# Making x's normal form again on GpSimd for the backward rows, with two of w1's loads issued later

## The chip, the cores and the metric

The kernel runs on one core of a Trainium2 chip. Its time is the device time of one execution in microseconds (us). The median of three runs before the change is 361.34 us (360.67 to 362.02). Engines are named as in the profile: PE is TensorE, PEld its weight loads, DVE is VectorE, ACT is ScalarE, POOL is GpSimd, SP is SyncE. SP does no arithmetic here, it only issues DMAs; POOL and ACT issue some too.

## The reference

The kernel computes the forward and the backward pass of a two-part mixer on x, of 2048 rows and 448 columns in bf16:

```
h  = x + irfft2(rfft2(layernorm(x)) * (w_r + i w_i))
h2 = h + transpose(gelu(layernorm(h)^T @ w1 + b1) @ w2 + b2)
```

w1 is 2048x1792 and w2 is 1792x2048. The outputs are h2 and, for a given grad_out, the gradients of x, w_r, w_i, w1, b1, w2 and b2. The layernorm has no weights: each row has its mean taken off and is divided by the root of its variance. The result of layernorm(x), called x's normal form here, is needed twice: as the input of the forward transform, and at the very end, where the gradient is taken back through the first layernorm (a product with the normal form, and a sum of it).

## The kernel before

Rows are dealt to partitions so that partition q holds rows 16q to 16q+15; a tile [128, 16, 448] holds x, and "row h" of the loops is x[:, h, :], 128 rows at once.

**Front (to about 95 us).** x is loaded in four chunks of four rows each (`load_x`, L255), grad_out in two (L292). `Norm.stats` and `Norm.finish` (L316 to L346) take mean and variance of each row on DVE, a square root on ACT, then `rstd` and `nb` (minus mean times rstd) on DVE, and make the normal form xln = x * rstd + nb, some rows on ACT (L345) and some on DVE (L342). `fft_rows` (L362) folds each group of four rows on DVE (L365, L366) and multiplies by a small table on PE (L376). `fft_cols` (L380), `cmul`, `ifft_cols`, `rows_mid` and `rows_out` are the rest of the transform. In the gaps of that chain PE works on `dg(j)` (L531), j = 0 to 13: grad_out times a transposed block of w2, called w2T. Each block comes by a transposing DMA into one of four buffers; `dg(j)` ends by issuing the load of block j+4 (`load_w2T`, L284).

**Order of the loads.** `nxt` (L202) keeps a list, `chain`: each load that goes through it is issued on SP right behind the one before it, so the order in the code is the order in SP's queue, and a load that must wait for its buffer holds all that are behind it. In this order stand: x, grad_out and the first w2T blocks; the tables; hi, di0, kinv, ident (L548 to L552); four stores of the normal form to DRAM, `xln_d` (L553, L554); block 8, block 9, and then what the loop of L594 to L599 issues: the store of the spectrum xs to DRAM (`xs_d`) behind product 6, and the first three chunks of w1 (`load_w1c`, L587, each two DMAs) behind products 5, 9 and 13. A chunk of w1 goes into a big buffer that earlier data must have left.

**Middle (95 to 230 us).** `gelu_in`, `gelu_out`, `gelu_back`, the product with w2 (L691), and the product with w1 transposed (L748), with the second layernorm's backward. PE works without a break here.

**Backward rows (about 280 to 336 us).** After the backward transform's columns the loop of L842 goes through 16 rows. For each one PE makes the row (`rows_mid_twice`, `rows_out`), and `norm_back` (L707) takes it back through the first layernorm, reading x's normal form from a tile `xr` (two buffers of four rows each, loaded from `xln_d` by POOL's queue every fourth row, L846, L847). The result gx is stored by POOL. Between the rows stand products of the weights' gradients: `gw2` (L762) and `gw1` (L801), whose results go from PSUM to tiles s6 and s4 (four buffers together, tag w4) and out by POOL's queue. From row 10 on `grad_w` adds DVE work.

**What sets the order.** The framework orders each engine's instructions at build time by their place in the code and by when it reckons them ready; `tc.issue_after` adds an order by hand. On the chip each engine runs its own list in that order and waits on semaphores. The loads of xr have no order by hand.

Of the kernel before, what the change touches and what calls it, by code (L numbers as in the profile page):

```python
# [11 lines left out]
BF16 = mybir.dt.bfloat16  # L12
F32 = mybir.dt.float32
ALU = mybir.AluOpType
# [3 lines left out]
P = 128  # L18
S = 2048
D = 448  # L20
# [3 lines left out]
NT = 16  # L24
# [111 lines left out]
def kernel(  # L136
# [21 lines left out]
    ve, ac, po, pe = nc.vector, nc.scalar, nc.gpsimd, nc.tensor  # L158

    consts = ctx.enter_context(tc.tile_pool(name="consts", bufs=1))  # L160
# [3 lines left out]
    dram = ctx.enter_context(tc.tile_pool(name="dram", bufs=1, space=bass.MemoryType.DRAM))  # L164

    def slot(i, shape, name):
        return big.tile(shape, BF16, tag=f"s{i}", name=name)
# [7 lines left out]
    def k1(shape, name, dtype=BF16):  # L175
        return ring.tile(shape, dtype, tag="k1", bufs=10, name=name)
# [4 lines left out]
    def col(n, name, dtype=F32):  # L181
        return ring.tile([P, n], dtype, tag=name, bufs=4, name=name)
# [7 lines left out]
    def ld(out, in_, eng=None):  # L190
        return (eng or nc.sync).dma_start(out=out, in_=in_)

    def st(out, in_, eng=None):
        return (eng or po).dma_start(out=out, in_=in_)  # L194
# [7 lines left out]
    def nxt(load, *args):  # L202
        if chain:
            with tc.issue_after(chain[-1].ins):
                chain.append(load(*args))
        else:
            chain.append(load(*args))
# [41 lines left out]
    def rows(ap):  # L249
        return ap.rearrange("(q h) d -> q h d", h=NT)  # L250
# [22 lines left out]
    def table(shape, src, tag=None):  # L273
        t = consts.tile(shape, BF16, name=src, **({"tag": tag} if tag else {}))
        nxt(ld, t[:], hnd[src].ap())
        return t
# [26 lines left out]
    rstd_x = consts.tile([P, NT], F32, name="rstd_x")  # L303
# [1 line left out]
    gb1 = consts.tile([P, NFB], F32, name="gb1")  # L305
    gb2 = consts.tile([P, NT], F32, name="gb2")

    xln_d = dram.tile([P, NT, D], BF16, name="xln_d")
    xs_d = dram.tile([P, 2, XW], BF16, name="xs_d")
    hn_d = dram.tile([S, D], BF16, name="hn_d")  # L310
    hln_d = dram.tile([NT, P, D], BF16, name="hln_d")
# [4 lines left out]
    class Norm:  # L316
        def __init__(self, src, dst, rstd, eps_col, scale, nm):
            self.src, self.dst, self.rstd, self.eps_col, self.scale, self.nm = src, dst, rstd, eps_col, scale, nm

        def stats(self, h):  # L320
            if h % 4 == 0:
                self.mv = col(8, f"mv_{self.nm}")
            bs = col(6, f"bs_{self.nm}")
            ve.bn_stats(out=bs[:], in_=self.src[:, h, :])  # L324
            i = h % 4
            ve.bn_aggr(out=self.mv[:, 2 * i:2 * i + 2], in_=bs[:])
            if h % 4 == 3:
                self.finish(h // 4)

        def finish(self, g):  # L330
            mv = self.mv[:, :].rearrange("p (i c) -> p i c", c=2)
            r = self.rstd[:, 4 * g:4 * g + 4]
            sq = col(4, f"sq_{self.nm}")
            ac.activation(out=sq[:], in_=mv[:, :, 1], func=ACT.Sqrt, bias=self.eps_col[:], scale=self.scale)
            ve.reciprocal(out=r, in_=sq[:])
            nb = col(4, f"nb_{self.nm}")
            ve.scalar_tensor_tensor(out=nb[:], in0=mv[:, :, 0], scalar=-1.0, in1=r, op0=ALU.mult, op1=ALU.mult)
            for i in range(4):
                h = 4 * g + i

                if (i > 1 or g == 3) if self.nm == "x" else (i > 1 and g == 3):
                    ve.tensor_scalar(out=self.dst[:, h, :], in0=self.src[:, h, :], scalar1=self.rstd[:, h:h + 1],  # L342
                                     scalar2=nb[:, i:i + 1], op0=ALU.mult, op1=ALU.add)
                else:
                    ac.activation(out=self.dst[:, h, :], in_=self.src[:, h, :], func=ACT.Identity,  # L345
                                  scale=self.rstd[:, h:h + 1], bias=nb[:, i:i + 1])  # L346
# [137 lines left out]
    def rows_mid_twice(ab, itab, h):  # L484

        pq = ps_sp([P, 2, 2, 113])
        for i, (kind, c) in enumerate(((0, 0), (0, 1), (1, 1), (1, 0))):
            last = pe.matmul(pq[:, i // 2, i % 2, :], lhsT=ab[:, kind, c, h, :, :],
                             rhs=itab[:, 113 * i:113 * i + 113], start=True, stop=True)
        eo = k1([P, 2 * DF], "eo2")  # L490
        out = eo[:].rearrange("p (a d) -> p a d", a=2)
        od = f2([P, 2, 113], "od")
        ac.copy(out=od[:], in_=pq[:, :, 1, :])
        ve.tensor_tensor(out=out[:, :, 0:113], in0=pq[:, :, 0, :], in1=od[:], op=ALU.add)
        ve.tensor_tensor(out=out[:, :, 224:112:-1], in0=pq[:, :, 0, 0:112], in1=od[:, :, 0:112], op=ALU.subtract)
        return eo, last
# [13 lines left out]
    def rows_out(eo):  # L510
        py = ps_sp([P, D])
        pe.matmul(py[:, 0:DF], lhsT=kinv[:, 0, :], rhs=eo[:, 0:DF], start=True, stop=False)
        pe.matmul(py[:, DF:D], lhsT=kinv[:, 0, :], rhs=eo[:, 223:0:-1], start=False, stop=False)
        pe.matmul(py[:, 0:DF], lhsT=kinv[:, 1, :], rhs=eo[:, DF:2 * DF], start=False, stop=False)
        pe.matmul(py[:, DF:D], lhsT=kinv[:, 2, :], rhs=eo[:, DF + 223:DF:-1], start=False, stop=True)  # L515
        return py


    xln = slot(1, [P, NT, D], "xln")
    nx = Norm(x, xln, rstd_x, eps_x, 1.0, "x")  # L520
# [10 lines left out]
    def dg(j):  # L531
        pg = ps_mm([P, D])
        with tc.issue_after(folded[min(j - 1, 3)][0].ins) if j else nullcontext():
            for t in range(NT):
                pe.matmul(pg[:], lhsT=w2T[j][:, t, :], rhs=go_nat[:, t, :], start=(t == 0), stop=(t == NT - 1))  # L535
        ev(du[:, j, 0:D], pg[:], "a")
        load_w2T()
# [12 lines left out]
    di0 = table([P, 4 * DF], "di0", "di")  # L550
    kinv = table([P, 3, P], "kinv")
    ident = table([P, P], "ident")  # L552
    for g in range(4):  # L553
        nxt(ld, xln_d[:, 4 * g:4 * g + 4, :], xln[:, 4 * g:4 * g + 4, :])  # L554
    with tc.issue_after(folded[3][1].ins):
        neg(hf[:, 0, 2], hf[:, 0, 1])
    xs = slot(3, [P, 2, XW], "xs")
# [29 lines left out]
    def load_w1c(on):  # L587
        c = len(w1c)
        n = 512 if c < 3 else 256
        w1c.append(slot((2, 4, 6, 5)[c], [P, NT, n], f"w1c{c}"))  # L590
        for k in range(0, n, 256):
            on(ld, w1c[c][:, :, k:k + 256], w1v[:, :, 512 * c + k:512 * c + k + 256])

    for j in range(4, NFB):  # L594
        dg(j)
        if j == 6:
            nxt(ld, xs_d[:], xs[:])
        if j in (5, 9, 13):
            load_w1c(nxt)  # L599


# [83 lines left out]
    for t0 in range(0, NT, 4):  # L685
# [7 lines left out]
        for i in range(4):  # L693
# [3 lines left out]
                                    op0=ALU.add, op1=ALU.add)  # L697
# [9 lines left out]
    def norm_back(ps, mean, xhat, rstd_c, back, base, out):  # L707

        v = f2([P, D], "v")
        if mean:  # L710
            nm1 = col(1, "nm1")
            ac.activation(out=nm1[:], in_=ps[:, D:D + 1], func=ACT.Copy, scale=rstd_c)  # L712
            ac.activation(out=v[:], in_=ps[:, 0:D], func=ACT.Identity, scale=rstd_c, bias=nm1[:])
        else:
            ac.activation(out=v[:], in_=ps[:, 0:D], func=ACT.Copy, scale=rstd_c)
        nm2 = col(1, "nm2")
        junk = k1([P, D], "junk")
        ve.tensor_tensor_reduce(out=junk[:], in0=v[:], in1=xhat, scale=back, scalar=0.0,
                                op0=ALU.mult, op1=ALU.add, accum_out=nm2[:])
        ve.scalar_tensor_tensor(out=junk[:], in0=xhat, scalar=nm2[:], in1=v[:], op0=ALU.mult, op1=ALU.add)  # L720
        ve.tensor_tensor(out=out, in0=junk[:], in1=base, op=ALU.add)
# [96 lines left out]
    def gw1_four(h):  # L818
        outs, out = gw1(h, ps_mm)
        outer(outs[:2], outs[2:], hlnT, du_t)  # L820
        out()
# [20 lines left out]
    for h in range(NT):  # L842
        if h + 2 < NT:
            mids.append(rows_mid_twice(ab2, di1, h + 2))
        if h % 4 == 0:
            xr = ring.tile([P, 4, D], BF16, tag="xr", bufs=2, name="xr")  # L846
            ld(xr[:], xln_d[:, h:h + 4, :], po)  # L847
        with tc.issue_after(mids[-1][1].ins):
            py = rows_out(mids[h][0])
        gx = k1([P, D], "gx")  # L850
        norm_back(py, False, xr[:, h % 4, :], rstd_x[:, h:h + 1], -1.0 / D, dh[:, h, :], gx[:])
        st(rows(out_1[0])[:, h, :], gx[:])
        if h < 8:
            gw2(h + 6, "aaav")
        else:
            gw1_four(h - 8)
        if h == 7:
            ld(xs_b[:], xs_d[:])
        if h > 9:
            grad_w(R_GROUPS[h - 10])  # L860

    for h in range(8, NT, 2):
        outs, out = gw1(h, ps_mm)
# [34 lines left out]
```

## Time and profile before

| | us |
|---|---|
| median of three runs | 361.34 (360.67 to 362.02) |
| the profiled execution's own time | 361.35 |
| its span, from the first instruction to the last | 359.5 |
| PE busy | 334.7 (93% of the span) |
| DVE busy | 243.9 (68%) |
| ACT busy | 210.5 (59%) |
| POOL busy, almost all of it issuing DMAs | 58.1 (16%) |

| stretch, us | PE busy | DVE busy | DMA, GB/s |
|---|---|---|---|
| 0 to 10.9 | 0.02 | 5.59 | 276 |
| 10.9 to 27.5 | 16.02 of 16.60 | 14.12 | 245 |
| 27.5 to 55.2 | 27.54 of 27.70 | 16.94 | 293 |
| 55.2 to 59 | 0.26 of 3.80 | 2.17 | 276 |
| 59 to 73 | 14.00 of 14.00 | 12.53 | 284 |
| 73 to 95 | 21.25 of 22.00 | 15.34 | 262 |
| 280 to 310 | 29.62 of 30.00 | 26.02 | 216 |
| 310 to 335 | 24.74 of 25.00 | 21.70 | 240 |

A line of a view of waits reads: who waited, for whom, us in total, how many times, the longest. A line of a timeline reads: start and length in us, engine, line of the code, operation, what it writes and reads, how often, and in brackets how long the engine stood idle before it and what ended that. A line of a tile's view gives the shortest, the median and the longest duration in ns. SPq is SP's queue of issues. For a DMA the view of its tile also gives the time from issue to landing; landing times below are the issue's start and that time added.

Landings in the front, in us: x's four chunks 4.77, 8.34, 14.45, 15.81; grad_out's two 7.22 and 10.83; w2T block 0 12.69, blocks 1 to 4 17.81, 21.14, 23.07, 25.93; ident 49.39; the four stores to xln_d 50.45, 51.52, 52.60, 53.77; block 8 58.69; the first two xr loads 57.19 and 58.68.

### The profile page before, as it was taken

How to read it: one execution, taken by the hardware profiler on the slowest of the kernel's cores; microseconds unless marked ns; L12 is line 12 of the kernel's file. 1: busy time of each engine (PE TensorE's matmuls, PEld its weight loads, DVE VectorE, ACT ScalarE, POOL GpSimd, SP SyncE). 2: the span in 40 equal slices, each digit the busy share in tenths (PEclk: the TensorE clock that was granted, in tenths of full speed). 3: DMA queues.
4: the chain of work that ended last, by engine and by line, in shares of the span. 5: the costliest groups of instructions: out<-in, count | busy, mean ns of one | idle time of the engine just before them, and what ended most of it. 6: DMA issues, size and time to landing. Idle time of an engine off the chain costs nothing.

```text
span 359.5 us, 5818 instructions
## 1 busy us (share of the span) xinstructions
PE 334.7 (93%) x2100; PEld 184.9 (51%) x2115; DVE 243.9 (68%) x580; ACT 210.5 (59%) x429; POOL 58.1 (16%) x106
## 2 busy tenths in 40 slices
PE   0799996999999999999999999989999999999994
PEld 0456664666664555555555555544555545454442
DVE  4883776967773999822226887837799997599600
ACT  2574653446658999304703344678766666677573
POOL 1000010001113011330160000010100243335620
PEclk9999999999999999999999999999999999999998
DMA  8999999999699999999999888599293365956664
GB/s 280 265 230 335 241 282 279 283 259 299 206 332 263 320 330 261 319 354 312 214 241 217 173 181 164 201 213 200 89 250 99 142 234 188 352 195 249 239 255 154
DMA packets 132988, 87.18 MB, mean 243 GB/s; under 512 B 92032, under 2 KB 124032, under 8 KB 132576
## 3 DMA queue, kind: packets, MB, share of 16 engines
q1 hardware_dynamic: 124768, 56.48, 65.8%
q0 software_dynamic: 8048, 30.31, 23.4%
q8 instruction: 16, 0.26, 0.3%
q14 instruction: 12, 0.10, 0.1%
q10 hardware_dynamic: 144, 0.03, 0.0%
HBM read 32.52 MB, written 30.76 MB: 176 GB/s over the span
## 4 chain that ended last, share of the span: by engine, by line
PE 71%; DVE 12%; ACT 7%; DMA 7%; issue 2%; ACTq 0%; DVEq 0%
PE ps_mm L224 13%; PE ps_mm L748 12%; PE ps_mm L622 6%; PE ps_sp L691 6%; PE ps_mm L691 6%; DMA w2T<-in_B_w_dram 6%; PE ps_mm L535 6%; PE ps_sp L622 5%; PE ps_mm L231 3%; PE ps_sp L224 2%; ACT s L243 2%; DVE bs_x L324 1%; PE ps_sp L405 1%; ACT zt L243 1%; PE ps_sp L376 1%
## 5 line engine op out<-in xcount | busy, mean ns | idle before, releaser
L243 ACT CAST s<-ps_mm 128x512 bf16<-128x512 f32 x96 | 48.4, 568 | 20.1 <-PE ps_mm L231 13.1
L535 PE MATMUL ps_mm<-go_nat,w2T 128*128 128x448 bf16 x224 | 50.9, 361 | 4.1 <-DMA w2T<-in_B_w_dram 4.1
L748 PE MATMUL ps_mm<-du,w1T 128*128 128x449 bf16 x224 | 43.4, 353 | 0.0
L224 PE MATMUL ps_mm<-goT,g_t 128*128 128x512 bf16 x158 | 41.2, 379 | 0.6 <-issue 0.3
L691 PEld LDWEIGHTS <-w2c 128*128 128x128 bf16 x224 | 21.9, 98 | 20.5
L748 PEld LDWEIGHTS <-w1T 128*128 128x128 bf16 x224 | 21.7, 97 | 20.7
L622 PEld LDWEIGHTS <-w1c 128*128 128x128 bf16 x224 | 21.8, 98 | 19.9 <-issue 1.0
L535 PEld LDWEIGHTS <-w2T 128*128 128x128 bf16 x224 | 21.8, 99 | 20.0 <-DMA w2T<-in_B_w_dram 5.4
L691 PE MATMUL ps_sp<-gT,w2c 128*128 128x448 bf16 x112 | 30.3, 352 | 0.0
L691 PE MATMUL ps_mm<-gT,w2c 128*128 128x448 bf16 x112 | 30.3, 352 | 0.0
L224 PE MATMUL ps_mm<-du_t,hlnT 128*128 128x512 bf16 (+1 forms) x141 | 30.1, 352 | 0.3 <-issue 0.2
L224 PEld LDWEIGHTS <-hlnT 128*128 128x128 bf16 x192 | 17.8, 98 | 20.5 <-issue 5.1
L426 DVE TENSOR_TENSOR gg<-ps_sp,gi 128x450 bf16<-128x450 f32 (+1 forms) x28 | 16.6, 642 | 16.8 <-ACT gi L423 16.8
L194 POOL DMA_DIRECT2D out_dram<-s x29 | 15.6, 538 | 62.6 <-ACT s L243 51.3
L622 PE MATMUL ps_mm<-hln,w1c 128*128 128x448 bf16 x112 | 23.8, 352 | 0.3 <-ACT hln L345 0.3
L712 ACT ACTIVATE nm<-ps_mm,rstd_h 128x1 f32<-128x1 f32 x16 | 4.2, 262 | 33.8 <-PE ps_mm L748 33.8
L224 PEld LDWEIGHTS <-g_t 128*128 128x128 bf16 x168 | 15.1, 97 | 15.5 <-issue 3.9
L622 PE MATMUL ps_sp<-hln,w1c 128*128 128x448 bf16 x112 | 22.8, 352 | 0.0
L696 DVE SCALAR_TENSOR_TENSOR h<-ps_mm,b2col,hr 128x448 bf16<-128x448 f32 x8 | 5.1, 680 | 25.8 <-PE ps_mm L691 25.8
L703 ACT ACTIVATE junk<-go_r 128x448 bf16<-128x448 bf16 x16 | 9.2, 576 | 18.4 <-DMA go_r<-in_grad_out_dram 18.0
L243 ACT CAST zt<-ps_sp 128x512 bf16<-128x512 f32 x26 | 13.4, 596 | 6.9 <-PE ps_sp L376 6.9
L578 DVE TENSOR_TENSOR x<-ps_sp,x 128x448 bf16<-128x448 f32 x16 | 10.0, 625 | 9.5 <-PE ps_sp L515 8.6
(157 smaller groups left out, 661.5 us busy)
## 6 DMA issues: line engine op xcount, KB each, us to landing
w1c<-in_B_w_dram SPq DMA_DIRECT2D x7, 1024.0 KB, 7.0
w2c<-in_B_w_dram SPq DMA_DIRECT2D x8, 896.0 KB, 12.4
out_dram<-s POOLq DMA_DIRECT2D x14, 512.0 KB, 3.0
out_dram<-s POOLq DMA_DIRECT2D x15, 448.0 KB, 3.0
xs_d<-xs SPq DMA_DIRECT2D x1, 1800.0 KB, 7.4
xs_b<-xs_d SPq DMA_DIRECT2D x1, 1800.0 KB, 9.9
x<-in_A_x_dram SPq DMA_DIRECT2D x4, 448.0 KB, 4.3
go_nat<-in_grad_out_dram SPq DMA_DIRECT2D x2, 896.0 KB, 7.3
```

Source lines behind the costliest of these rows:

```text
L194: return (eng or po).dma_start(out=out, in_=in_)
L224: last = pe.matmul(ps, lhsT=lhs[:, c, a], rhs=rhs[:, c, b], start=opens and c == 0, stop=not opens and c == 2)
L231: last = pe.matmul(ps, lhsT=lhs[k, 3, a], rhs=rhs[k, 3, b], start=opens, stop=not opens)
L243: return ac.copy(out=out, in_=in_)
L426: last = ve.tensor_tensor(out=out, in0=by_k(pr), in1=by_k(gi), op=op)
L535: pe.matmul(pg[:], lhsT=w2T[j][:, t, :], rhs=go_nat[:, t, :], start=(t == 0), stop=(t == NT - 1))
L578: ve.tensor_tensor(out=hn[:, h, :], in0=py[:], in1=x[:, h, :], op=ALU.add)
L622: pe.matmul(pu[:], lhsT=wc[:, h, o:o + P], rhs=hln[:, h, :], start=(h == 0), stop=(h == NT - 1))
L691: pe.matmul(p2[i][:], lhsT=w2c[t0 // 4][:, j, i * P:(i + 1) * P], rhs=gT[:, j, :], start=(j == 0), stop=(j == NFB - 1))
L696: ve.scalar_tensor_tensor(out=h2[:], in0=p2[i][:], scalar=b2col[:, t:t + 1], in1=hr[:, i, :], op0=ALU.add, op1=ALU.add)
L703: ac.activation(out=junk[:], in_=go_r[:, h, :], func=ACT.Copy, accum_out=gb2[:, h:h + 1])
L748: w1_last = pe.matmul(pd[:], lhsT=w1T[:, j, :], rhs=du[:, j, 0:D + 1], start=(j == 0), stop=(j == NFB - 1))
```

## The change

The store of the normal form and its DRAM tensor go. `nb`, which was a small tile of its own for each group of four rows, becomes part of one tile that lasts to the end (and the same for the second layernorm). The load of `xr` reads x itself from its place among the inputs, in the same layout and of the same size (448 KB), and four tensor_scalar instructions on POOL turn it, in place, into the normal form: times rstd, plus nb, row by row. Apart from that, the first chunk of w1 is issued behind product 7 instead of 5, and the second behind product 10 instead of 9.

```diff
-    xln_d = dram.tile([P, NT, D], BF16, name="xln_d")
...
             self.src, self.dst, self.rstd, self.eps_col, self.scale, self.nm = src, dst, rstd, eps_col, scale, nm
+            self.nb = consts.tile([P, NT], F32, name=f"nb_{nm}")
...
-            nb = col(4, f"nb_{self.nm}")
-            ve.scalar_tensor_tensor(out=nb[:], in0=mv[:, :, 0], scalar=-1.0, in1=r, op0=ALU.mult, op1=ALU.mult)
+            nb = self.nb[:, 4 * g:4 * g + 4]
+            ve.scalar_tensor_tensor(out=nb, in0=mv[:, :, 0], scalar=-1.0, in1=r, op0=ALU.mult, op1=ALU.mult)
...
     ident = table([P, P], "ident")
-    for g in range(4):
-        nxt(ld, xln_d[:, 4 * g:4 * g + 4, :], xln[:, 4 * g:4 * g + 4, :])
...
         dg(j)
         if j == 6:
             nxt(ld, xs_d[:], xs[:])
-        if j in (5, 9, 13):
+        if j in (7, 10, 13):
             load_w1c(nxt)
...
             xr = ring.tile([P, 4, D], BF16, tag="xr", bufs=2, name="xr")
-            ld(xr[:], xln_d[:, h:h + 4, :], po)
+            ld(xr[:], rows(A_x[0])[:, h:h + 4, :], po)
+
+            for i in range(h, h + 4):
+                po.tensor_scalar(out=xr[:, i - h, :], in0=xr[:, i - h, :], scalar1=rstd_x[:, i:i + 1],
+                                 scalar2=nx.nb[:, i:i + 1], op0=ALU.mult, op1=ALU.add)
```

## The prediction

> **What bounds the kernel now.** I read the page's rows of tenths first, then TensorE's waits up to 60 us, then the SyncE and GpSimd queues in order of time. Two rows of the page:
>
> ```profile
> PE   0799996999999999999999999989999999999994
> DMA  8999999999699999999999888599293365956664
> ```
>
> A slice is 9 us. TensorE (PE) is at nine tenths or more nearly everywhere, and the DMA engines are full for the first 99 us. A saved transfer or a freed engine is therefore worth only what it takes out of a PE gap. The gaps up to 60 us, from the waits of PE:
>
> ```profile
> PE ps_sp L376 <- DVE eo L370: 10.9, 1, 10.9
> PE ps_mm L535 <- DMA w2T<-in_B_w_dram: 3.5, 1, 3.5
> PE ps_sp L376 <- DVE rstd_x L335: 0.4, 1, 0.4
> PE ps_sp L376 <- ACT du L243: 0.2, 1, 0.2
> ```
>
> PE has nothing to do until the first normalised and folded rows of x exist (10.9 us), and stands 3.5 us for one w2T block; the same wait once more, between 60 and 100 us, is 0.6 us. The two small waits (23.45 and 26.43 us) say that up to 26 us PE is just as far as VectorE (DVE) lets it be: a delay there has no cover. From 27.5 to 55.2 us PE is busy 27.54 of 27.70 us, from 112 to 185 us 73.00 of 73.00, from 280 to 310 us 29.62 of 30. Why the w2T block is late, from SyncE's order of time:
>
> ```profile
> 40.11 0.57 SPq L191 DMA_DIRECT2D hi<-tab_hi  x1
> ...
> 42.83 2.79 SPq L191 DMA_DIRECT2D xln_d<-xln  x4
> 47.45 10.71 SPq L197 DMA_TRANSPOSE w2T<-in_B_w_dram  x2
> 58.33 2.27 SPq L191 DMA_DIRECT2D w1c<-in_B_w_dram  x2
> 60.65 8.26 SPq L197 DMA_TRANSPOSE w2T<-in_B_w_dram  x1
> 69.01 0.52 SPq L191 DMA_DIRECT2D xs_d<-xs  x1
> ```
>
> The four stores of x's normal form stand right ahead of the ninth block (w2T number 8, issued at 47.45). Its window in the tile's view gives 11.2 us to landing, at 58.69; PE had done product 7 at 55.2. The stores landed at 50.45, 51.52, 52.60 and 53.77: one each 1.1 us, in turn, with the block behind them. And GpSimd's (POOL's) queue:
>
> ```profile
> 1.92 0.54 POOL L191 DMA_DIRECT2D b2r<-in_B_b_dram  x1
> 50.73 0.57 POOL L191 DMA_DIRECT2D xr<-xln_d  x1 [48.27 <-DMA xln_d<-xln]
> 51.81 0.55 POOL L191 DMA_DIRECT2D xr<-xln_d  x1 [0.50 <-DMA xln_d<-xln]
> ```
>
> The first two loads of xr are that queue's third and fourth DMAs, in line from 2.46 us and held only by the stores. They then run at 50.73 to 58.68, beside block 8.
>
> **The change, part by part.**
>
> *Stores removed.* Four SyncE issues (2.79 us) and 1.8 MB go. The block's issue moves from 47.45 to about 43, and its data no longer waits for landings that end at 53.77 but for ident's at 49.39: 4.4 us. Blocks 1 to 4 landed 17.81, 21.14, 23.07, 25.93, some 2 to 3 us apart, block 8 4.9 us behind the last store, since it shared with the xr loads; so about 2 us more. It should land near 52.4, 2.8 us ahead of 55.2. The gap of 3.54 us closes; what is late next is computed with the moved loads.
>
> *Moved loads.* Queue before, behind block 8: 9, w1's first chunk (two of 1 MB), 10, xs_d, 11, 12, 13, second chunk. After: 9, 10, xs_d, 11, first chunk, 12, 13, second chunk. The second chunk keeps its place, as products 10 to 13 issue no load. Block 10 comes forward. New is that xs_d heads the queue for block 11: it waits for xs's last eviction (about 60 us before, 57 after with the gap closed). By their spacings (xs_d 5.4 us, a block 2.4, half a chunk 4.6) xs_d lands near 63, block 11 at 65.5, the chunk at 75, block 12 at 77, 13 at 79.5. Product 11 starts at 78.88 before, 75 after; product 12 near 81, 13 near 85; the chunk is first read at 95, then 91. All have 4 us or more, so the second gap (0.56) closes too. Without that cover it costs what it is, 0.6. Gain: 3.54 + 0.56 = 4.1.
>
> *The early xr loads.* Nothing holds them now, so they leave at 2.5 and 3.0 us: 0.9 MB, into the stretch in which x, grad_out and w2T arrive at full rate (5 to 10 us: mean 379 GB/s, DMA at nine tenths or more). That is 2.4 us of transfers. b1r, a few KB issued at 1.28 on the same queue, landed at 6.33, so xr moves from about 6 us: x's first chunk (4.77) escapes, the second (8.34) comes about 1 us later, the third (14.45) about 2, and the first w2T block (12.69) about 2. DVE reads them in order:
>
> ```profile
> 14.83 0.62 DVE L324 BATCH_NORM_STATS2 bs_x<-x 128x6 f32<-128x448 bf16 x1
> 15.65 0.63 DVE L365 TENSOR_TENSOR eo<-xln 128x892 bf16<-128x892 bf16 x1 [0.21 <-ACT xln L345]
> ```
>
> The statistics at 14.83 need the third chunk, which had 0.4 us to spare, and the fold of the second group stands behind them: the fold comes 1.2 to 1.9 us later, and PE's chain with it. Bounds: 0, if the loads only fill holes (not less: no transfer ahead of 40 us goes), and 2.4, the whole transfer; I take 1.4, as the third chunk had a little to spare and the loads must start late enough to miss the first. PE's own delay by the first block is smaller: its first eight products there are 0.375 us apart and from 15.7 us on 0.19, so a later start costs less if it is by then fast.
>
> *GpSimd's arithmetic.* Sixteen tensor_scalar on 128x448 bf16. No such row on POOL exists; the nearest are the same work on DVE and on ScalarE (ACT), first two lines, and POOL's only elementwise rows, two memsets: 0.10 us for one element, 0.15 for 64.
>
> ```profile
> L342 DVE TENSOR_SCALAR xln<-x,rstd_x,nb_x x10: 379/392/398, 8.1 to 24.6; 128x448 bf16<-128x448 bf16 x10
> L345 ACT ACTIVATE xln<-x,nb_x,rstd_x x6: 744/754/760, 8.1 to 21.4; 128x448 bf16<-128x448 bf16 x6
> ```
>
> The memsets' slope (0.05 us for 63) gives 0.46 us; twice ACT's row, 1.5, is my upper end. I take ACT's 0.75, as it too makes one element per lane and step. On POOL itself this is idle time: eight at about 10 to 19 us, where POOL waits anyhow until 82. What is queued behind is hn_d. The question is whether they slow DVE. No row shows POOL arithmetic beside DVE. Below: 0, and no gain, as DVE keeps all its own work. Above: every one holds DVE for its length, 8 x 0.75 = 6.0 us. I take 0.5: only folds that meet one wait, and the first group falls on statistics. Front in all: 1.4 + 0.5 = 1.9 later.
>
> *The backward rows.* xr's third load leaves at 292.17 and landed at 297.29. The four tensor_scalar wait for it on POOL, then take 3.0: to 300.3. Rows are first read by row 8 at 306.06: 5.8 us of cover. Behind them wait gx and s stores of 293.93, 294.78, 296.81 and 298.33; s of 294.78 goes out near 300.9, lands 3.0 later, at 303.9, and the fourth s tile after it, which reuses its buffer, is begun near 306: 2 us left. The fourth load (303.88, landed 307.90) has until 324.22. DVE idles 0.6 to 0.7 us a row there, which hides waits of one POOL instruction a row. I take 0.2; ends 0 and 2 (if the buffer margin is gone).
>
> *nb's tile* is written by the same DVE instruction (0.16 us): nothing.
>
> Sum: -4.1 + 1.9 + 0.2 = -2.0 us. The profiled execution took 361.35 us (span 359.5), the median of three is 361.34: no correction. 361.35 - 2.0 = 359.35, say 359.4.
>
> The Trainium skill speaks against this change: SBUF — State Buffer, § Who interferes with whom, has GpSimd share a port pair with VectorE as an exclusive lock, where a VectorE instruction with two SBUF inputs and a GpSimd instruction that reads SBUF exclude each other and the loser "fully blocks". By it the folds (two inputs from xln) wait for whole POOL instructions, and the sum goes toward the slow rival below. No run here shows it yet.
>
> **Rivals.**
>
> *The whole gain (0.20).* The loads of xr fill holes (the DMA row of a window from 10 to 15 us has digits of 6, 3 and 5 near 10.5) and DVE isn't held: 361.35 - 4.1 = 357.3. Against it: 379 GB/s from 5 to 10 us leaves little.
>
> *POOL holds DVE (0.20), slower.* Place: groups 0 and 1, 10 to 19 us, where DVE's chain is PE's. Eight instructions of 0.75 each hold DVE for their length: +6.0, with 1.4 of late x and 0.2 behind: 361.35 - 4.1 + 7.6 = 364.9. It decides from the point at which the holds pass 2.5 us (4.1 - 1.4 - 0.2), 0.31 us for each instruction. For it: a quarter of a microsecond is less than any price above. Against: the statistics, about half of DVE's work there (16 of 0.6 us), read one input, and DVE needn't meet each.
>
> *The gap only moves (0.10).* xs_d at the queue's head makes block 11 or 12 late, or block 8 is slow by itself: PE waits again for what it gains, and the time stays about 361.4. Against: 4 us of cover or more in each step.
>
> **How the numbers follow.** The forecast's own case has 0.50, from 358 to 361, half of it below 359.5. A measurement of this kernel tells 0.5% (1.8 us) from no change: faster means below 359.5, slower above 363.1. Faster: 0.25 + 0.20 = 0.45. Slower: the hold, 0.20 less 0.03 for a mild one, and 0.03 for a backward stall that takes the 2 us on top of a bad front: 0.20. Same: the other 0.35. The range reaches from the whole gain, 357.0, to 363.5, where most of the holding case is left out.
>
> **What would show it.** Right: no wait for w2T at 55 to 59 us nor at 79; xr loads issued before 4 us; x's third chunk landing at 16 to 17; PE's first fold product (10.9) up to 1.5 us later and product 4's stretch some 2 us later; POOL rows near 0.75 us; no new PE gap after 280 us. Wrong: DVE's folds (0.63) or tensor_scalars (0.39) lengthened while POOL works, xr loads issued late, a w2T wait at block 11 or 12, s evictions waiting for a POOL store near 306 us.

## The result, and the profile after

| | before, us | after, us |
|---|---|---|
| median (22 runs of each) | 362.03 (360.55 to 364.94) | 360.79 (359.37 to 361.75) |
| profiled execution, its own time | 361.35 | 360.13 |
| its span | 359.5 | 358.0 |
| last w2T product ends | 94.90 | 93.56 |
| last product of all ends | 354.80 | 353.58 |

The ratio is 0.9955 (95%: 0.9935 to 0.9974). It is that of the means, 360.70 to 362.35; the medians differ by 1.24 us. Ratios here and below leave out runs that took over 1.5% more than the fastest of their kernel, and they need not be the quotient of the medians. The kernel became a little faster, by 1.2 us where 2.0 had been forecast, and within the 0.5% that counts here as no change. In the profiled pair the gain stands whole at the end of the w2T products (-1.34) and is nearly the same at the end (-1.22): it arose in the first 95 us and the backward rows took back 0.1 (the difference is still -1.34 at 275 us and -1.23 at 302).

The page's two rows of tenths, after:

```profile
PE   0499999999999999999999999989999999999995
DMA  7999995999599999999699978498293364966654
```

The 6 in PE's seventh slice (54 to 63 us) is now a 9, and the second slice fell from 7 to 4: one gap was closed and another, at the start, grew. The waits of PE up to 60 us give the sizes:

```profile
PE ps_sp L376 <- DVE eo L370: 13.3, 1, 13.3
PE ps_mm L535 <- DMA w2T<-in_B_w_dram: 0.7, 2, 0.4
```

The first line was 10.9, the second a single 3.5. From 60 to 100 us no wait for w2T is left (0.6 before). -3.54 - 0.56 + 2.43 (first line) + 0.41 (the longer wait of the second, which ends at 40.18 us, for block 5) = -1.26, which is the -1.34 of the table within 0.1. SyncE's queue, in order of time, shows the new order of the loads:

```profile
45.23 9.86 SPq L197 DMA_TRANSPOSE w2T<-in_B_w_dram  x3
60.07 0.32 SPq L191 DMA_DIRECT2D xs_d<-xs  x1
60.49 6.38 SPq L197 DMA_TRANSPOSE w2T<-in_B_w_dram  x1
66.97 3.34 SPq L191 DMA_DIRECT2D w1c<-in_B_w_dram  x2
```

Block 8 is the first of the three issued from 45.23, and it landed at 52.39, ahead of PE. GpSimd's queue:

```profile
2.45 1.12 POOL L191 DMA_DIRECT2D xr<-in_A_x_dram  x2
10.05 3.62 POOL L848 TENSOR_SCALAR xr<-xr,rstd_x,nb_x 128x448 bf16<-128x448 bf16 x4 [6.47 <-DMA xr<-in_A_x_dram]
16.71 3.76 POOL L848 TENSOR_SCALAR xr<-xr,rstd_x,nb_x 128x448 bf16<-128x448 bf16 x4 [3.04 <-DVE nb_x L337]
```

The two loads of xr leave from 2.45 us on, as nothing holds them now, 278 us ahead of the first row that reads the tile, at 280. What that does shows in the chain that ended last. Its longest pieces in the first 14 us, before and then after:

```profile
0.74 4.03 DMA x<-in_A_x_dram
4.79 1.15 DVE bs_x L324 x2
...
8.12 1.42 ACT xln L345 x2
9.56 0.63 DVE eo L365
```

```profile
1.66 9.32 DMA x<-in_A_x_dram
11.04 0.51 issue
11.54 1.08 DVE eo L365
12.62 0.54 DVE eo L366
```

Before, the chain began with x's *first* chunk, landed at 4.77, and went through the statistics to the first fold (L365) at 9.56. After, it begins with the *second* chunk, which landed at 10.98 instead of 8.34. On VectorE:

```profile
8.70 0.70 DVE L342 TENSOR_SCALAR xln<-x,rstd_x,nb_x 128x448 bf16<-128x448 bf16 x2
11.00 0.63 DVE L324 BATCH_NORM_STATS2 bs_x<-x 128x6 f32<-128x448 bf16 x1 [1.60 <-DMA x<-in_A_x_dram]
11.54 1.08 DVE L365 TENSOR_TENSOR eo<-xln 128x892 bf16<-128x892 bf16 x1
12.55 0.61 DVE L366 TENSOR_TENSOR eo<-xln 128x892 bf16<-128x892 bf16 x1
```

One statistics instruction of the second chunk stands ahead of the first fold in VectorE's order. VectorE idled 1.60 us for its data, and the fold, whose last input ScalarE had finished at 10.12, waited behind it. The fold itself, from 11.54, runs beside POOL's first group (from 10.05 to 13.67) and takes 1.08 us instead of 0.63. The second fold runs beside the same group and keeps its length (0.61 us, 0.62 before).

x's third and fourth chunk came later for another reason, their issue: SyncE's issue of w2T block 0, which stands ahead of them, lasted 10.39 us instead of 7.61, and they left at 13.44 and 14.06 instead of 10.69 and 11.30.

### The profile page after: what moved, and what is told of

It reads as the page before. It is cut to its first block, busy times and chain, and to the rows that moved or that the text cites. A ratio compares the mean times of both kernels' runs of the same rounds, so it can differ in the third digit from the quotient of the medians.

```text
span 358.0 us, 5854 instructions
## 1 busy us (share of the span) xinstructions
PE 336.0 (94%) x2115; PEld 185.1 (52%) x2115; DVE 246.0 (69%) x580; ACT 210.6 (59%) x429; POOL 72.2 (20%) x122
## 4 chain that ended last, share of the span: by engine, by line
PE 73%; DVE 11%; DMA 8%; ACT 5%; issue 1%; SPq 1%; ACTq 0%; DVEq 0%
PE ps_mm L224 13%; PE ps_mm L746 12%; PE ps_mm L535 6%; PE ps_mm L620 6%; PE ps_mm L689 6%; PE ps_sp L689 6%; PE ps_sp L620 5%; DMA hlnT<-hln_d 3%; DMA w2T<-in_B_w_dram 3%; DMA x<-in_A_x_dram 3%; PE ps_mm L231 2%; PE ps_sp L224 2%; PE ps_sp L459 2%; PE ps_sp L376 1%; PE ps_sp L460 1%; PE ps_sp L405 1%
## 5 line engine op out<-in xcount | busy, mean ns | idle before, releaser
L224 PE MATMUL ps_mm<-goT,g_t 128*128 128x512 bf16 x168 | 43.0, 379 | 0.0
L426 DVE TENSOR_TENSOR gg<-ps_sp,gi 128x450 bf16<-128x450 f32 (+1 forms) x28 | 16.6, 643 | 16.5 <-ACT gi L423 16.5
L376 PE MATMUL ps_sp<-kf,eo 128*128 128x128 bf16 x64 | 5.1, 243 | 13.8 <-DVE eo L370 13.3
```

What stands on the lines that cost most here:

```text
L224: last = pe.matmul(ps, lhsT=lhs[:, c, a], rhs=rhs[:, c, b], start=opens and c == 0, stop=not opens and c == 2)
L376: last = pe.matmul(pz[:, c, :], lhsT=eo[:, i, o:o + P], rhs=kf[:], start=True, stop=True)
L426: last = ve.tensor_tensor(out=out, in0=by_k(pr), in1=by_k(gi), op=op)
```

## The experiments

My theory after the result: the change closes a gap of 4.1 us, and its loads of xr at 2.5 us, with the arithmetic behind them, give 2.8 of it back in the front. Rivals: the order of w1's loads brings or takes something; POOL's hold on VectorE is the larger part; the early loads are harmless and the front's loss has another cause. A further one came up on the way, the clock that is granted to PE. Each ratio is against runs of the kernel before on the same chip. Their median was 362.79 us (31 runs) beside the first four kernels below, 362.78 (17) beside the late loads on SyncE's queue, the moved stores, the longer wait and the held loads, and 361.72 (17) beside the other three.

**The first two xr loads late, on POOL's queue.** Edit of the changed kernel; the loads and their arithmetic come behind the last store of h2 on POOL.

```diff
-            ld(xr[:], rows(A_x[0])[:, h:h + 4, :], po)
+            with tc.issue_after(h2_last.ins):
+                ld(xr[:], rows(A_x[0])[:, h:h + 4, :], po)
```

> The changed kernel with the first two loads of xr and their eight GpSimd instructions held behind the last store of h2 on GpSimd's own queue (about 185 us), where nothing on TensorE waits for them. My theory (the early loads of xr delay x and the first w2T blocks by 2.4 us and GpSimd holds VectorE for 0.45 us, and that is all that the change gives back): TensorE's first folded product comes back from 13.31 to 10.9 us, no wait for w2T at 55 us, and the time is 2.4 to 2.9 us under the changed kernel, ratio to the kernel before about 0.988. Rival (the gain was only the 1.3 us that is seen, because the DMA engines or later stages bound the rest): within 0.5 us of the changed kernel.

Measured: ratio 1.0041 (0.9997 to 1.0086), 364.60 us in the profiled execution. The front does what was expected: the first folded product starts at 10.46 us (13.31 after the change) and the w2T products end at 90.86, 2.70 earlier. It is lost again mainly at one place, shown by PE's waits between 180 and 230 us:

```profile
PE ps_mm L746 <- DMA w1T<-in_B_w_dram: 4.6, 1, 4.6
```

The xr loads were issued at 184.10 and 184.64, in the same microsecond as a block of w1 transposed (184.06), and landed at 190.32 and 196.40; that block landed at 196.59, and PE, now earlier, wanted it at 192. In the changed kernel it had landed at 192.14. From 197.0 to 200.4 PE's granted clock was 0.50. So the front's price is confirmed, and my expectation of the whole failed on a new collision. Its twelve runs went from 360.70 to 375.56 us, with mean clocks from 1.0 down to 0.975.

**The order of w1 alone, from both sides.** In the changed kernel the old places of the chunks; in the kernel before the new ones.

```diff
-        if j in (7, 10, 13):
+        if j in (5, 9, 13):
```

> The changed kernel with the first two chunks of w1 issued behind products 5 and 9 again, so that the first chunk stands ahead of w2T block 10 in SyncE's queue. My theory (the removed store does the work, the order of w1 is only a cover): block 10 and 11 land up to 9 us later, at most one short wait for w2T of 0 to 0.6 us near 77 us, and the time is 0 to 0.6 us over the changed kernel. Rival (the order of w1 makes the gain): 1.3 us over the changed kernel or more, level with the kernel before.

> The kernel before with the two chunks of w1 issued behind products 7 and 10, and nothing else. My theory: the wait of 3.5 us at 55 to 59 us stays, as block 8 still stands behind the four stores; only the wait of 0.56 us near 79 us goes: 0.4 to 0.6 us under the kernel before. Rival (the order of w1 makes the gain): 1.3 us under it or more.

Measured: with the old order the changed kernel has ratio 0.9953 (0.9933 to 0.9974), the same as with the new one; blocks 10 and 11 landed at 69.45 and 75.45 without a wait. The new order in the kernel before has 0.9989 (0.9963 to 1.0015): the wait at block 8 stays (3.81 us in its profile), the second gap goes. The moved chunks thus carry no part of the change's gain as it stands that these runs can show.

The first of the two has the front of the changed kernel in another execution, and it lost its time elsewhere: x's second chunk landed at 9.92, the first folded product started at 12.18, and then PE stood 1.1 us for block 0 (landed at 15.12) and 0.4 for block 5. The w2T products ended at 94.13 all the same. How the front's loss divides between x and the blocks thus varies from one execution to the next.

The profile of the second also showed something I had no term for. Its windows (us, PE, PEld, DVE, ACT, POOL busy, then the granted clock, DMA share, GB/s):

```profile
55.00:59.70 4.70, 0.90 (x5) 0.28 (x3) 3.08 (x6) 0.73 (x2) 0.00 (x0) 0.83 1.19 304
59.70:65.00 5.30, 5.29 (x19) 2.83 (x20) 2.60 (x5) 1.07 (x2) 0.00 (x0) 0.50 0.88 235
65.00:70.00 5.00, 5.00 (x39) 3.58 (x38) 3.89 (x7) 2.14 (x4) 0.00 (x0) 1.00 1.01 305
```

Behind the wait PE ran at half clock, 19 matmuls in 5.30 us where the next 5.00 us hold 39. A wait can cost more than its length.

**Without POOL's arithmetic.** The changed kernel without the 16 tensor_scalar; x stands in place of its normal form in the last gradient, so that output differs.

> The changed kernel without the sixteen GpSimd instructions: xr holds x itself, so the gradient of x is taken with x in place of its normal form; all else is the same. My theory: VectorE's first fold takes 0.63 us instead of 1.08 and the first folded product comes at about 12.9 instead of 13.31 us; in the backward rows nothing; the time is 0.3 to 0.6 us under the changed kernel. Rival (GpSimd's hold on VectorE is most of what is given back): 2 us under the changed kernel or more, with the first folded product near 11 us.

Measured: ratio 0.9947 (0.9926 to 0.9968), profiled 359.34 (0.8 under the changed kernel's), w2T products end at 92.86 (0.70 earlier). The first folded product starts at 11.01, earlier than expected, since x's second chunk landed at 9.15 in this execution. But PE then stood for something else; its waits up to 60 us:

```profile
PE ps_sp L376 <- DVE eo L370: 11.0, 1, 11.0
PE ps_mm L535 <- DMA w2T<-in_B_w_dram: 1.7, 1, 1.7
```

That is w2T block 0, landed at 14.53. So the early loads delay two things, x and the first block, and taking one away uncovers the other. By the two profiles the difference is 0.7 to 0.8 us, part of which may be x's second chunk, 1.83 us earlier in this execution; by the ratios it can't be told from nothing. The rival that the hold is the larger part is out.

**The loads late on SyncE's queue.** The changed kernel; the first two loads of xr behind those of w_b, at 219 us, clear of w1's blocks. Their arithmetic follows at once.

```diff
+    for g in range(2):
+        xrs.append(ring.tile([P, 4, D], BF16, tag="xr", bufs=2, name="xr"))
+        with tc.issue_after(wb_loads[-1].ins):
+            ld(xrs[g][:], rows(A_x[0])[:, 4 * g:4 * g + 4, :])
```

> The changed kernel with the first two loads of xr issued by SyncE behind the last load of w_b (about 222 us), where the transposed blocks of w1 have all been issued, and their eight GpSimd instructions following at about 230 us. My theory (the early loads and the hold on VectorE are all that is given back; the late place of the run before failed since it stood in front of the fourth block of w1, needed 8 us later): first folded product at 10.4 to 10.9 us, no wait of TensorE over 0.5 us before 230 us, granted clock 0.997 or more, 2.4 to 2.9 us under the changed kernel, ratio to the kernel before 0.985 to 0.990. Rival (any place for these loads costs about the same): within 0.7 us of the changed kernel.

Measured: ratio 0.9928 (0.9902 to 0.9955), profiled 359.63. The front is right again (first folded product 10.57, w2T products end at 90.34, 3.2 us ahead of the changed kernel's), and only 0.5 of it is left at the end. Where it went: POOL, in order of time, and then VectorE.

```profile
226.75 8.13 POOL L857 TENSOR_SCALAR xr<-xr,rstd_x,nb_x 128x448 bf16<-128x448 bf16 x8 [43.20 <-DMA xr<-in_A_x_dram]
```

```profile
229.23 1.02 DVE L365 TENSOR_TENSOR eo<-go_r 128x892 bf16<-128x892 bf16 x1
230.18 0.61 DVE L366 TENSOR_TENSOR eo<-go_r 128x892 bf16<-128x892 bf16 x1
...
231.91 1.01 DVE L355 TENSOR_TENSOR e<-eo 128x896 bf16<-128x896 bf16 x1
```

The same lines of the changed kernel, where POOL does nothing at that place:

```profile
231.86 0.63 DVE L365 TENSOR_TENSOR eo<-go_r 128x892 bf16<-128x892 bf16 x1
...
233.76 0.63 DVE L355 TENSOR_TENSOR e<-eo 128x896 bf16<-128x896 bf16 x1
```

The eight instructions fell on the fold of the backward transform, where PE has nothing else to do. Again not every fold was slowed (L366 kept 0.61). PE's wait there and the windows around it:

```profile
PE ps_sp L376 <- DVE e L355: 2.0, 1, 2.0
```

```profile
229.74:233.16 3.42, 1.43 (x10) 0.58 (x10) 3.17 (x7) 0.52 (x1) 3.42 (x4) 1.00 1.16 254
233.16:236.57 3.41, 3.41 (x26) 2.04 (x24) 0.69 (x1) 2.51 (x5) 2.82 (x5) 0.50 1.06 237
```

Right after the wait, which ends at 232.97, come 3.4 us at half clock, in which up to 1.7 us of PE's work is lost. Between 230 and 260 us the lead over the changed kernel shrank from 3.23 to 0.63 us.

**The arithmetic later still.** The same kernel, with the eight instructions behind the store of b1's gradient, past that fold.

```diff
+            with tc.issue_after(sr_last.ins):
```

> The run e5 with the eight GpSimd instructions of the first two groups moved once more, behind the store of b1's gradient (about 235 us), past the last fold of the backward transform's input. Theory: in e5 these instructions stood beside that fold on VectorE and stretched it by 2 us, TensorE waited 2.0 us and its clock fell to half for 3.4 us. Moved, the wait at 233 us and the half clock after it go: 2 to 3.5 us under e5, 356.5 to 358 us, ratio to the kernel before 0.982 to 0.988. Rival (the loads behind w_b were what made it late): the wait at 233 us stays, within 0.7 us of e5.

Measured: ratio 0.9891 (0.9856 to 0.9926), median 358.18. The wait at 233 is gone, the clock at 0.998 in the profile. The arithmetic isn't quite free there either: VectorE's products ahead of L426 are held (one of L442 took 0.98 us, 0.62 in the changed kernel), and PE's waits for L426's results between 225 and 262 us are 1.5 us in all, 0.8 in the changed kernel. With its loads and its arithmetic out of the two places where VectorE sets PE's pace, the change is worth 1.1%. It is the same computation as the changed kernel's: what the changed kernel gives away, it gives away by where these instructions stand.

**The stores kept, only moved.** Kernel before; the four stores go behind w2T block 10's load, and w1's chunks stand as in the changed kernel. No arithmetic on POOL.

```diff
-    for g in range(4):
-        nxt(ld, xln_d[:, 4 * g:4 * g + 4, :], xln[:, 4 * g:4 * g + 4, :])
...
         if j == 6:
+            for g in range(4):
+                nxt(ld, xln_d[:, 4 * g:4 * g + 4, :], xln[:, 4 * g:4 * g + 4, :])
             nxt(ld, xs_d[:], xs[:])
-        if j in (5, 9, 13):
+        if j in (7, 10, 13):
```

> The kernel before, with its stores and loads of the normal form kept, but the four stores moved behind w2T block 10 in SyncE's queue (and w1's chunks behind products 7 and 10). My theory (the wait at 55 us comes from the place of the stores; the 1.8 MB still have to pass): no wait at block 8; the stores run in the slack before the store of xs, xr's loads follow, block 11 lands 3 to 6 us later than in the changed kernel (70.5), and TensorE waits 0.5 to 3 us near 75 us; granted clock 0.996 or more; 1 to 3 us under the kernel before. Rival (the transfers themselves must go): level with the kernel before, within 0.5 us.

Measured: ratio 0.9872 (0.9836 to 0.9908), median 358.03, with one of six runs at 363.06. Block 8 landed at 50.75 and block 11 at 70.98; the wait that I expected at block 11 didn't come. PE's one wait for w2T was 1.1 us for block 5, ahead of all that the edit touches. SyncE's queue:

```profile
43.22 10.23 SPq L197 DMA_TRANSPOSE w2T<-in_B_w_dram  x3
53.55 3.14 SPq L191 DMA_DIRECT2D xln_d<-xln  x4
57.88 0.32 SPq L191 DMA_DIRECT2D xs_d<-xs  x1
58.29 10.76 SPq L197 DMA_TRANSPOSE w2T<-in_B_w_dram  x1
```

The xr loads still hang behind the stores (issued at 57.69, landed at 67.26 and 69.25), so they stay out of the front without any order by hand.

**The same with w1's chunks in their old places, and a repeat.**

> The run e6 (stores of the normal form behind block 10) with w1's first chunks issued behind products 5 and 9 as in the kernel before, so that the first chunk stands ahead of block 10 and of the stores. Theory: 2 MB, 4.6 us each half, come ahead of blocks 10 and 11, and the stores with xr's loads behind them: block 11 lands near 80 us, product 11 would start near 75: a wait of 2 to 6 us near 75 us, 2 us or more over e6. Rival (w1's order does not matter here either): within 0.7 us of e6.

> The kernel of e6 again, beside e10 on one chip, to see which of the two ways is the faster one. Theory: no wait over 1.2 us before 230 us in either; e6 has no GpSimd arithmetic and no hold of VectorE but 1.8 MB more to store; the two lie within 1 us, ratio to the kernel before 0.984 to 0.990.

Measured: 1.0070 (1.0047 to 1.0092) with the old order, 0.9893 (0.9858 to 0.9929) with the new one, medians 364.08 and 357.87 on one chip. PE's waits from 40 to 100 us with the old order:

```profile
PE ps_mm L535 <- DMA w2T<-in_B_w_dram: 4.3, 1, 4.3
```

It ends at 79.98, for block 11, with half clock from 79.9 to 83.3. With the stores in the queue there, the place of w1's chunks is worth 6.2 us; in the changed kernel, which has no stores, it is worth nothing that the runs show. Two parts of an edit can't always be priced one by one: the chunks alone gave 0.9989, the stores alone 1.0070, both together 0.9872 and 0.9893. Beside the repeat, the kernel with the arithmetic later (358.18) can't be told apart.

**A longer wait.** Kernel before with one store more, of 448 KB to a DRAM tensor that nobody reads, ahead of block 8, to see what a longer gap does to the clock.

> The kernel before with one store more, 448 KB of the normal form to a DRAM tensor that nothing reads, behind the four and ahead of w2T block 8. Theory of the clock (a wait of TensorE of some 3.5 us or more lets its granted clock fall to half for some microseconds; the kernel before stands at the edge of it): the wait grows by 1.1 us to about 4.6, the granted clock falls to half after it in nearly every execution (mean 0.985 to 0.991), and the time grows by 2 to 3.5 us. Rival (the wait costs only its length): 1.1 us more, mean clock as in the kernel before (0.994).

Measured: ratio 1.0095 (1.0066 to 1.0124). The wait grew from 3.5 to 6.75 us, more than expected, because block 8 now shared its whole time with the xr loads and landed 7.1 us behind the last store. The windows:

```profile
55.50:62.20 6.70, 0.00 (x0) 0.00 (x0) 2.15 (x5) 0.53 (x1) 0.00 (x0) 0.73 1.19 207
62.20:65.40 3.20, 3.17 (x11) 1.64 (x12) 0.89 (x2) 0.86 (x2) 0.00 (x0) 0.50 0.86 208
```

The w2T products end 4.33 later than in the kernel before: 3.2 of wait, 1.6 for 3.2 us at half clock, less the second gap's 0.56: 4.2. All its runs had a mean clock of 0.985 to 0.990.

**The xr loads held, the stores left in place.** Kernel before; the two loads wait on POOL for the last store of hln, and are issued at 113.4 us.

```diff
+            with tc.issue_after(hln_last.ins):
+                ld(xr[:], xln_d[:, h:h + 4, :], po)
```

> The kernel before with its first two loads of xr held behind the last store of the second normal form on GpSimd's queue (about 111 us), so that they no longer run beside w2T block 8; stores and the order of w1 as before. My theory (4.4 us of the block's delay are the stores, about 2 us the xr loads, and a wait under 3 us keeps the clock): block 8 lands near 56.7, TensorE waits 1.2 to 2.0 us for it instead of 3.5, granted clock 0.997 or more, 2 to 3.5 us under the kernel before. Rival (the loads beside the block cost nothing, the stores do all): wait 3 us or more, within 0.7 us of the kernel before.

Measured: ratio 0.9892 (0.9864 to 0.9920), median 359.71. But its twelve runs go from 356.82 to 367.30, and the quotient of the means of all runs is 0.996, so how much this kernel gains stays open. In the profile no wait at block 8 is left: it landed 2.87 us behind the last store, where it had taken 4.92. The neighbours' share of 2.05 agrees with the prediction's "about 2 us more". The wait of 1.2 to 2.0 that I expected to remain didn't show, as ident and the stores also landed 2 us earlier in this execution (ident at 46.97, 49.39 before). A new one came behind it, as PE arrived 4.65 us earlier at w1's transposed blocks (185 to 200 us):

```profile
PE ps_mm L748 <- DMA w1T<-in_B_w_dram: 2.2, 1, 2.2
```

That place is where the first kernel lost its gain too. Whether it is also what spreads these runs is not shown, as no long one was profiled.

## Why the prediction came out nearly right

The forecast was 359.4 from a profiled execution of 361.35; that of the changed kernel took 360.13, and its median is 360.79, inside the range (357.0 to 363.5). The sum gave -2.0 and the profiles -1.2. The mechanism held; one term of the sum was too small, and a second wait behind it and the clock were missing. One reading was off without touching the sum: the page's DMA row is at 6 tenths from 90 to 99 us, so the engines were not full for all of the first 99.

- **Stores removed: right.** Block 8 forecast at 52.4, landed at 52.39; the 3.54 closed. That the landing agrees so closely is luck: ident landed at 50.73 instead of 49.39, and the block 1.66 us behind it instead of the 3.0 that the forecast amounts to.
- **Moved loads: right in what mattered.** The 0.56 closed, and no wait came at blocks 10 to 13. Landings were later than forecast (xs_d 67.15 for 63, block 11 70.46 for 65.5, the first chunk 76.20 for 75, blocks 12 and 13 78.29 and 80.39 for 77 and 79.5) and the cover was needed: block 11 used 5.0 of its forecast 9.5 us. That the moved chunks gain nothing here came out only in the run with the old order.
- **The early xr loads: the step that was too small, 1.4 forecast, 1.98 measured.** I let x's first chunk escape, gave the second 1 us and the third 2, and read the third as the one that matters. The chunks came 0.6, 2.6, 2.9 and 2.6 later. It was the second, for a reason that stood in the trace of before: VectorE takes a statistics instruction of the second chunk ahead of the first fold. Of the 1.98, 0.58 is the first chunk's delay, and 1.40 came by the second. The upper end of 2.4 held. These are figures of one execution: with the same loads the second chunk landed at 9.92 in the kernel with the old order and at 9.15 in the one without arithmetic.
- **The first w2T block: its delay forecast, not its sequel.** It came 2.75 later (15.44; "about 2" forecast), and the chain of blocks with it: block 5 was issued at 29.69 instead of 25.84 and landed at 40.13 instead of 37.12, PE stood 0.41 for it. Ahead of 27 us the trace had shown no cover; between 27.5 and 55.2 I took PE's 27.54 of 27.70 for a stretch that no late block touches, without asking how late the blocks already were: in the profile of before block 5 landed at 37.12 and its product began at 37.16. The 0.41 is not the early loads' alone, though. In four of ten profiles without early loads PE stood 0.66 to 1.23 us for block 5, in the other six 0.3 at most.
- **GpSimd's arithmetic: right in size, wrong in place, so the size is in part luck.** 714 ns each by the median (704 to 1532; 0.75 forecast) and 0.45 us in the front (0.5 forecast). I expected the first group to fall on statistics. It fell on the first fold, 0.63 to 1.08, because the fold had been pushed to 11.54 by the late chunk; the tensor_scalars of the second group (0.70 to 1.03 for two, though each reads one tile) are no loss, as ScalarE's half of that group ends later.
- **The backward rows: right,** 0.1 for 0.2. POOL's lines of xr's tile, and VectorE beside the third group of four (296.07 to 299.8):

```profile
L848 POOL TENSOR_SCALAR xr<-xr,rstd_x,nb_x x16: 704/714/1532, 10.0 to 312.5; 128x448 bf16<-128x448 bf16 x16
```

```profile
295.86 0.69 DVE L244 CAST s<-ps_mm 128x512 bf16<-128x512 f32 x1 [0.57 <-PE ps_mm L224]
296.49 0.39 DVE L494 TENSOR_TENSOR eo<-ps_sp,od 128x226 bf16<-128x226 f32 x1
...
297.99 1.01 DVE L718 SCALAR_TENSOR_TENSOR junk<-xr,nm,v 128x448 bf16<-128x448 bf16 x1
299.04 1.04 DVE L719 TENSOR_TENSOR gx<-junk,go_r 128x448 bf16<-128x448 bf16 x1
```

  L718 and L719 read two tiles in SBUF and went from 0.69 and 0.39 to 1.01 and 1.04; L244 and L494, which read PSUM (L494 one tile in SBUF besides), kept their 0.69 and 0.39. VectorE's idle time there took it, PE was busy 29.77 of 30 us.
- **The rival "POOL holds DVE" (364.9)** was right that they hold each other and wrong that the chain meets most of it: one fold of 0.45, not 6.0. The Trainium skill (SBUF — State Buffer, § Who interferes with whom) names this pair, a VectorE instruction with two SBUF inputs beside a GpSimd one that reads SBUF. It says that the two contend, under a rule that contention is an exclusive lock; its words "fully blocks" stand beside another case, VectorE's two-port modes. The folds of 1.08 and 1.02 us and the unchanged PSUM readers agree with it. What neither the rival nor my sum had is that the two take turns: in the front the fold waited for the end of one GpSimd instruction (at 12.15), and then the next one waited for both folds, the second of which lost nothing.

```profile
12.14 1.53 POOL L848 TENSOR_SCALAR xr<-xr,rstd_x,nb_x 128x448 bf16<-128x448 bf16 x1
```

  How much is lost depends on where the instructions fall: the same arithmetic cost some 0.45 in the front, helped to lose some 2.6 us at 229 us, and 0.1 in the backward rows.
- **Not in the sum: the granted clock.** In the profiled pair it plays no part (0.997 in both). In the runs it does: the changed kernel had a mean clock of 0.997 to 1.0 in all 22, the kernel before 0.989 to 0.998 in the 65 runs beside the experiments. In the 31 runs of the kernel before beside the first four kernels, the seven with a clock of 0.991 or less took 364.2 us on average, the nineteen from 0.992 to 0.995 362.6, and the five from 0.996 on 361.3. Its wait at block 8 is at the edge at which the clock falls, so closing it also closes something that the profile of before, one with a whole clock, does not show. How the -1.2 of the medians divides into this and the rest stays open: the clocks of the 22 runs of before in that pair are not known, and both profiled executions were 0.7 us under their medians.

A gain of about the 4.1 us of the first rival was to be had, but not by this placing: by the ratios, the stores moved (0.9872 and 0.9893) and the loads and arithmetic later (0.9891) took 3.9 to 4.6 us off their kernels before. A part of that is the clock, which was under 0.996 in 24 of the 34 runs of the kernel before that they are compared with. The two ways can't be told apart, so in these runs remaking the normal form on GpSimd brings nothing that moving its store doesn't.

## What to carry to other kernels

When an edit takes away the store that a load had to wait for, it also takes away what kept that load out of a crowded stretch: ask where in its queue it will now start, and put it by hand. Read the order of instructions on the engine that sets the pace, not only the transfer times: one statistics instruction ahead of the first fold turned a late second chunk into 2 us. And price a gap of a few microseconds on PE at its length and the slow clock that may come with it.

## What the runs showed of the hardware

PE's waits of 3.81, 4.32, 4.56 and 6.75 us each brought a granted clock of 0.50, for 3.4 to 6.8 us; one of 3.54 in the profile of before and one of 2.22 in the kernel with the held xr loads did not, and with the loads late on SyncE's queue one of 2.0 was enough. The length of the wait thus doesn't decide. In these traces each stretch at half clock between two at full clock lasts 3.41 us (three of them) or 6.83 (two), so I cut each trace into steps of 3.41 us from its changes of the clock. In the step ahead of the fall PE was busy for 0.00, 0.30, 0.31, 1.19 and 1.43 us. At each kernel's end, where the clock falls too, it was 1.03 or less. The emptiest step at full clock that no fall followed has 1.49: it is in the kernel before, whose one wait of 3.54 lies across two steps:

```profile
53.40:56.81 3.41, 1.79 (x12) 0.89 (x10) 3.41 (x7) 1.33 (x3) 0.00 (x0) 1.00 1.12 349
56.81:60.23 3.42, 1.49 (x11) 1.02 (x12) 0.56 (x1) 0.52 (x1) 0.00 (x0) 1.00 1.12 200
```

The wait of 3.81 lies otherwise: its first step, from 54.71 to 58.13, has 1.19, and the clock fell at 58.13, before the wait was over. By these figures the fall comes behind a step in which PE is busy for less than some 1.45 us of 3.41 (between 1.43 and 1.49). Where the steps lie against a wait differs from one execution to the next, which would explain why runs of the kernel before differ in their clock; that is not shown, as only one of its runs has a trace. The Trainium skill (TensorE: Matmul & The Clock Gate, § Part 1: The HAM clock gate) has half clock come after at least one idle window of about 3.4 us, in windows that run freely. The steps agree with it, but here windows with 1.19 and 1.43 us of work were idle enough.

GpSimd pays for the sharing as well: its tensor_scalar of 0.71 us came at one each 1.02 us (8.13 for eight) beside VectorE's fold, and the longest, held by two folds, took 1.53.

At the start 0.9 MB of loads that nobody needed yet, issued from 2.45 us on by another engine, made x's second chunk, grad_out's two and w2T block 0, all issued by SyncE at the same times as before, land 2.6 to 2.8 us later (in two other profiles with these loads, 0.8 and 1.6 for the chunk and 1.8 and 2.4 for block 0): here issuing from another engine did not keep the transfers apart.
